# Convolving two entering chunks in one set of matmuls, with tiles of two for x and the partial sums

## The chip, the cores and the metric

The kernel runs on one core of a Trainium2 chip. The metric is the device time of one execution in microseconds. The kernel before takes 1448.68 us (median of three runs, 1447.93 to 1449.42).

## The reference

Two layers follow each other on `x` of shape (8, 4224, 192): batch `b`, token `s`, channel `d`.

```python
# 1: causal convolution along the tokens, 7 taps, one softmax-normalised set of taps per head (8 heads of 24 channels)
x = einsum('hk,bskhg->bshg', softmax(weight), windows_of_7(x))
# 2: phase layer
theta = x @ w_theta
zr, zi = x * cos(theta), x * sin(theta)
y = einsum('ts,bsd->btd', w_tok_r, zr) + einsum('ts,bsd->btd', w_tok_i, zi)
u = x + y
out = u + relu(u @ w_ch)
```

Nearly all of the work is the token mix `y`: two products of 4224 x 4224 matrices with 4224 x 1536 data.

## The kernel before

**Chunks and steps.** The tokens that are summed over (`s`) are cut into 33 chunks of 128 tokens; the tokens of the output (`t`) into 33 blocks of 128. A chunk lives in an fp16 tile `z` (7 parts of 768 columns, 11 buffers), so at most 11 chunks are resident and there are three rounds of 11 chunks. The main loop runs over 58 steps. A step takes one pair of output blocks (step 6, 23, 40 and 57 take a single one) and multiplies it with all resident chunks: for a pair, seven runs over the chunks (`runs`, `mix`), each with a transposed or summed weight tile `wt`, two matmuls of 384 columns per run and chunk (line 443), accumulated in PSUM tiles `y`. At the end of some runs `give` adds `y` into the partial sums `pv` (line 408, VectorE), which are fp32 tiles of 128 x 1536, one per output block. After a step its `pv` go to a DRAM scratch `part` (line 456), and a round later they are read back (`load_rows`, line 372). In the last round they stay until the output is made of them (`output`, line 476).

**Entering chunks.** `start` says at which step a chunk becomes resident. In rounds two and three the chunks enter at steps 18 to 23 and 36 to 41, two at a time, except for one that enters alone at step 20 and one at step 38. Each of these chunks is prepared in the step before it enters. Two steps before, at position 4.5 of the step's seven, `load_chunk` makes the tile `xw` and issues its loads: 96 partitions hold four token quarters with 16 rows of history each, so that there are four loads of x (line 197, POOL's queue, float32 to fp16) and, for every chunk but the first of a round, four copies of history out of the `xw` of the chunk before it (line 188, SP's queue). `conv` then convolves the chunk by matmuls with banded matrices (line 210): two calls, each with eight matmuls of 192 columns (four heads, two halves of the partitions) and one evacuation by ScalarE of 128 x 768 (line 151). Then come the transpose, the two `theta` calls and the VectorE products and sums.

**The order.** `pe`, `dve`, `act` and `pool` chain the instructions of an engine in the order in which the program issues them. `step_events` gives every side task of a step a position on a scale of seven, and `mix` issues it when the matmuls of the step get there. For the first of two entering chunks the two `conv` calls stand at 0.1 and 0.6, for the second at 2.4 and 2.9. Loads of `xw` are not chained; the scheduler places them on POOL's queue, and its order is fixed at build time. An instruction that waits on a queue holds all that stand behind it on the same queue.

**The buffers.** `xw` and `pv` share one set of six buffers (tag "big", 6144 bytes on each partition); only the `pv` of steps 0 and 1 live elsewhere. A new tile gets a buffer whose old tile has been released, and its first write waits for the last readers of the old tile.

```python
self.xw = wk.tile([2 * WR, 2, B, D], F16, name="xw", tag="big", bufs=6)    # line 182
pv = wk.tile([P, N], F32, name="pv", tag="big", bufs=6)                   # line 370
found.append((1.6, steps[t + 1].load_rows))                               # line 518
found.append((4.5, lambda k=k: load_chunk(k)))                            # line 542, k that start at t + 2
```

Of the kernel before, what the change touches and what calls it, by code (L numbers as in the profile page):

```python
# [11 lines left out]
F16 = mybir.dt.float16  # L12
F32 = mybir.dt.float32
# [3 lines left out]
def kernel(  # L17
# [23 lines left out]
    nc = tc.nc  # L41
    B, S, D = x.shape
    H, KS = weight.shape
    G = D // H
    P = nc.NUM_PARTITIONS
    assert (B, D, P) == (8, 192, 128) and S % P == 0
    N = B * D
    HD = D // 2
    HN = N // 2
    NQ = 4  # L50
    Q = P // NQ
    NK = S // P
    NT = S // P
    HALO = 16
    WR = Q + HALO
# [5 lines left out]
    NW = 11  # L61
# [4 lines left out]
    start = [base[k % NW] + (NU + 1) * (k // NW) for k in range(NK)]  # L66
# [17 lines left out]
    def pe(ins):  # L84
        return in_order("pe", ins)

    def dve(ins):
        return in_order("dve", ins)

    def act(ins):  # L90
        return in_order("act", ins)

    def pool(ins):
        return in_order("pool", ins)

    constp = ctx.enter_context(tc.tile_pool(name="const", bufs=1))
    wk = ctx.enter_context(tc.tile_pool(name="wk", bufs=2))
    zpool = ctx.enter_context(tc.tile_pool(name="zpool", bufs=NW))
# [10 lines left out]
    xs = dram.tile([S, N], F16, name="xs")  # L109
    part = [dram.tile([NT, P, N], F32, name=f"part{i}") for i in range(2)]  # L110

    def banks(name, dtype=F32):
        return mmpool.tile([P, 2, PC if dtype == F32 else 2 * PC], dtype,
                           name=name, tag="mm")
# [5 lines left out]
    bands = constp.tile([2 * WR, H, 2, Q], F16, name="bands")  # L120
# [10 lines left out]
    def token(k, a):  # L131

        return (a * NK + k) * Q
# [13 lines left out]
    def evacuate(out, in_, by_dve=False):  # L147
        if by_dve:
            dve(nc.vector.tensor_copy(out=out, in_=in_))
        else:  # L150
            act(nc.scalar.activation(out=out, in_=in_, func=AT.Copy))  # L151
# [23 lines left out]
    Z11, T1, Z21, Z22, T2, T4, T3 = range(7)  # L175

    class Chunk:


        def __init__(self, k, before=None):  # L180
            self.k = k
            self.xw = wk.tile([2 * WR, 2, B, D], F16, name="xw", tag="big", bufs=6)
            for a in range(NQ):
                h, lo = a // 2, (a % 2) * WR
                t0 = token(k, a)
                hist = self.xw[lo : lo + HALO, h, :, :]
                if before is not None:
                    nc.sync.dma_start(
                        out=hist, in_=before.xw[lo + Q : lo + Q + HALO, h, :, :]
                    )  # L190
                elif t0 == 0:
                    nc.vector.memset(hist, 0.0)
                else:
                    lo, t0 = lo - HALO, t0 - HALO
                lo += HALO
                n = (a % 2 + 1) * WR - lo
                nc.gpsimd.dma_start(  # L197
                    out=self.xw[lo : lo + n, h, :, :],
                    in_=x[:, t0 : t0 + n, :].rearrange("b s d -> s b d"),
                )  # L200

        def conv(self, j):

            if j == 0:
                self.z = zpool.tile([P, 7, HN], F16, name="z", tag="z")
                self.x = self.z[:, T2 : T2 + 2, :].rearrange("p t n -> p (t n)")
            pc = banks("pc")
            for h in range(4):
                for half in range(2):
                    pe(nc.tensor.matmul(  # L210
                        pc[half * 2 * Q : (half + 1) * 2 * Q, h // 2,
                           h % 2 * B * G : (h % 2 + 1) * B * G],
                        lhsT=bands[:, 4 * j + h, :, :].rearrange("p a m -> p (a m)"),
                        rhs=self.xw[:, half, :, (4 * j + h) * G : (4 * j + h + 1) * G],
                        start=True, stop=True,
                    ))
            evacuate(
                self.x.rearrange("p (b d) -> p b d", d=D)[
                    :, :, 4 * j * G : 4 * (j + 1) * G
                ].rearrange("p b (i h g) -> p i h b g", i=2, h=2),  # L220
                pc[:, :, 0 : 2 * B * G].rearrange("p i (h b g) -> p i h b g", h=2, b=B),
                self.k == 0 and j == 1,
            )
            if j == 1:
                for a in range(NQ):
                    t0 = token(self.k, a)
                    nc.sync.dma_start(
                        out=xs[t0 : t0 + Q, :], in_=self.x[a * Q : (a + 1) * Q, :]
                    )

        def transpose(self):
            self.xT = turned()
# [27 lines left out]

        def tasks(self):

            for j in range(2):
                yield lambda j=j: self.conv(j)
            yield self.transpose
            for g in range(NG):
                yield lambda g=g: self.theta(g)
            yield lambda: self.product(Z11)
            yield lambda: self.product(Z21)
            yield lambda: self.sums(0)  # L270
            yield lambda: self.sums(1)

    chunks = {}

    def load_chunk(k):
        if k < NK and k not in chunks:
# [8 lines left out]
    class Step:  # L285
# [79 lines left out]
        def load_rows(self):  # L365
            for tb in self.tbs:
                if self.t < 2:
                    pv = zpool.tile([P, N], F32, name="pv", tag="z")
                else:
                    pv = wk.tile([P, N], F32, name="pv", tag="big", bufs=6)  # L370
                if not self.first:
                    nc.sync.dma_start(
                        out=pv, in_=part[(self.t // NU - 1) % 2][tb, :, :]
                    )
                self.pv.append(pv)
# [137 lines left out]
    def step_events(t):  # L513
        found = []
        s = steps[t]
        if t + 1 < NSTEP:
            found += steps[t + 1].w_tasks()
            found.append((1.6, steps[t + 1].load_rows))
            for i in steps[t + 1].adds:
                found.append((2 + 2 * i, lambda i=i: steps[t + 1].load_x(i)))  # L520
                found.append((3.6 + 2 * i, lambda i=i: steps[t + 1].add_x(i)))
        here = [(r, i, which) for r in steps for i, when, which in r.ahead if when == t]
        for j, (r, i, which) in enumerate(here):
            found.append((1.5 + 1.8 * j, lambda r=r, i=i, which=which: r.add_ahead(i, which)))
        if t + 2 < NSTEP:
            nxt = steps[t + 2]
            for m in (1, 2):
                found.append((1.3 + 3 * (m - 1), lambda m=m: nxt.load_w(m)))
        if t == NU - 2:
            def load_wch():  # L530
                dve(nc.vector.memset(wch[:, 1:3, :], 0.0))
                for rows, i, part_w in channel_pieces(moe_w_ch):
                    pool(nc.gpsimd.dma_start(out=wch[rows, i, :], in_=part_w))
            found.append((3, load_wch))
        for at, f in outputs:
            begin = at - sum(s.time for s in steps[:t])
            if 0 <= begin < steps[t].time:
                found.append((7 * begin / steps[t].time, f))
        if t >= NU - 2:
            new = [k for k in range(NK) if start[k] == t + 2 and k >= NW]  # L540
            for k in new:
                found.append((4.5, lambda k=k: load_chunk(k)))
            at = 0.1
            for k in (k for k in range(NK) if start[k] == t + 1 and k >= NW):
                pos = [0, .5, 1.4, 2.2, 2.6, 3.1, 3.15, 3.4, 3.6]

                def add(at, j, k):
                    def go():
                        if j == 0:
                            chunks[k].todo = chunks[k].tasks()  # L550
                        next(chunks[k].todo)()
                    found.append((at, go))
                for j, p in enumerate(pos):
                    add(at + p, j, k)
                at += 2.3
        return found
# [12 lines left out]
    for a in range(2):  # L569
        nc.gpsimd.affine_select(  # L570
            out=sel, in_=sel, pattern=[[1, Q - 1 + 2 * WR]], channel_multiplier=-1,
# [4 lines left out]
    for a, lo in ((0, True), (1, False)):  # L576
        nc.gpsimd.affine_select(
            out=block[:, a : a + 1], in_=block[:, a : a + 1], pattern=[[0, 1]],
# [7 lines left out]
    def idle(n):  # L586
# [7 lines left out]
        out=wmax, in_=wsb, axis=mybir.AxisListType.X, op=ALU.max  # L594
    ))
    dve(nc.vector.tensor_tensor(
        out=wsb, in0=wsb, in1=wmax[:, :].unsqueeze(2).to_broadcast([P, H, KS]),
# [6 lines left out]
        out=wsum, in_=wsb, axis=mybir.AxisListType.X, op=ALU.add  # L604
# [5 lines left out]
        out=wdiag, in0=wsb[0:KS, :, :],  # L610
# [4 lines left out]
        out=wcol, in_=wdiag, axis=mybir.AxisListType.X, op=ALU.add  # L615
# [5 lines left out]
    for q in range(Q):  # L621
        pe(nc.tensor.matmul(
            bp[0 : 2 * WR, 0, q * H : (q + 1) * H],
            lhsT=sel[:, Q - 1 - q : Q - 1 - q + 2 * WR], rhs=taps,
            start=True, stop=True,
# [3 lines left out]
        out=bands, in0=bv.unsqueeze(2).to_broadcast([2 * WR, H, 2, Q]),  # L629
# [32 lines left out]
    for i in range(NW + 2):  # L662
        ch = chunks.get(i) if i < NW else None
# [80 lines left out]
```

## Time and profile before

| | before |
|---|---|
| median of three runs | 1448.68 us |
| span of the profiled execution, first to last instruction | 1444.6 us |
| what lies around the span (median less span) | 4.1 us |
| TensorE busy (PE) | 1414.5 us, 98% of the span |
| VectorE (DVE), ScalarE (ACT), GpSimd (POOL) busy | 978.2, 316.2, 434.6 us |
| matmuls of the token mix, line 443 | 7656, start to start 0.163 us |
| matmuls of the convolution, line 210 | 528 |
| mean granted TensorE clock | 0.997 |

The span is one profiled execution; its own time was not measured apart, so the median less the span stands for what lies around it. In the views, PE is TensorE's matmuls and PEld its weight loads, which overlap them; SPq is SP's DMA queue. A line of the timeline gives start, duration, engine, line, operation, output tile from input tile, count, and in brackets the idle time of the engine before it and what ended it. A step of 11 chunks takes 25.0 us in round two; the steps 17 to 22 and 35 to 39, in which chunks are prepared, take 26.7 us.

### The profile page before, as it was taken

How to read it: one execution, taken by the hardware profiler on the slowest of the kernel's cores; microseconds unless marked ns; L12 is line 12 of the kernel's file. 1: busy time of each engine (PE TensorE's matmuls, PEld its weight loads, DVE VectorE, ACT ScalarE, POOL GpSimd, SP SyncE). 2: the span in 40 equal slices, each digit the busy share in tenths (PEclk: the TensorE clock that was granted, in tenths of full speed). 3: DMA queues.
4: the chain of work that ended last, by engine and by line, in shares of the span. 5: the costliest groups of instructions: out<-in, count | busy, mean ns of one | idle time of the engine just before them, and what ended most of it. 6: DMA issues, size and time to landing. Idle time of an engine off the chain costs nothing.

```text
span 1444.6 us, 23749 instructions
## 1 busy us (share of the span) xinstructions
PE 1414.5 (98%) x9809; PEld 886.3 (61%) x9809; DVE 978.2 (68%) x1050; ACT 316.2 (22%) x379; POOL 434.6 (30%) x655
## 2 busy tenths in 40 slices
PE   7899999999999999999999999999999999999997
PEld 4656666666666666666666666666666666666665
DVE  6893554555448687866666657876877677767686
ACT  6851101111124254000000004435210110010133
POOL 8421211111223232432433343233323123213120
PEclk9999999999999999999999999999999999999999
DMA  9975756564699999897899889989999999898883
GB/s 181 253 148 136 146 119 133 98 152 87 152 229 210 226 244 222 219 265 173 223 245 222 233 155 239 235 181 237 274 220 202 213 204 221 204 200 193 166 232 116
DMA packets 272029, 281.99 MB, mean 195 GB/s; under 512 B 106672, under 2 KB 240176, under 8 KB 271920
## 3 DMA queue, kind: packets, MB, share of 16 engines
q0 software_dynamic: 162464, 92.15, 48.4%
q1 hardware_dynamic: 71824, 178.88, 35.2%
q10 hardware_dynamic: 37632, 9.44, 4.3%
q8 instruction: 77, 1.26, 0.4%
q14 instruction: 32, 0.26, 0.1%
HBM read 245.49 MB, written 108.13 MB: 245 GB/s over the span
## 4 chain that ended last, share of the span: by engine, by line
PE 89%; DVE 3%; DMA 2%; ACT 2%; POOL 1%; issue 1%; SPq 0%; DVEq 0%; ACTq 0%; POOLq 0%
PE y L443 81%; PE v L141 5%; PE pc L210 1%; PE tp L165 1%; ACT z L246 1%; DVE pv L408 1%; DMA xw<-xw 1%; POOL xw L197 1%; DMA xw<-in_x_dram 1%; DVE z L257 1%; POOL st L323 1%; DVE z L251 1%; DMA pv<-part 1%; ACT uT L151 1%; DVE wt L336 0%
## 5 line engine op out<-in xcount | busy, mean ns | idle before, releaser
L443 PE MATMUL y<-z,wt 128*128 128x384 f16 x7656 | 1283.6, 326 | 10.4 <-DVE pv L408 7.3
L443 PEld LDWEIGHTS <-wt 128*128 128x128 f16 x7656 | 740.7, 98 | 488.1 <-issue 10.2
L408 DVE TENSOR_TENSOR pv<-y,pv 128x768 f32<-128x768 f32 x324 | 309.2, 955 | 327.0 <-PE y L443 286.8
L336 DVE STREAM_TRANSPOSE wt<-st 128x1408 f16<-128x1408 f16 (+7 forms) x224 | 327.8, 1465 | 45.8 <-PE y L443 39.1
L323 POOL DMA_DIRECT2D st<-in_moe_w_tok_r_dram x232 | 132.4, 579 | 464.9 <-DVE wt L336 459.4
L323 POOL DMA_DIRECT2D st<-in_moe_w_tok_i_dram x232 | 132.5, 580 | 405.4 <-DVE wt L336 397.5
L348 DVE TENSOR_TENSOR wt<-wt 128x1408 f16<-128x1408 f16 (+7 forms) x216 | 176.1, 815 | 40.5 <-PE y L443 38.0
L151 ACT ACTIVATE z<-pc 128x768 f16<-128x768 f32 x65 | 53.3, 820 | 386.7 <-PE pc L210 386.5
L151 ACT ACTIVATE ub<-pv 128x768 f16<-128x768 f32 x63 | 50.2, 835 | 333.2 <-DVE pv L408 310.7
L406 ACT ACTIVATE pv<-y 128x768 f32<-128x768 f32 x66 | 54.0, 819 | 281.6 <-PE y L443 281.6
L141 PEld LDWEIGHTS <-uT 128*128 128x128 f16 x1056 | 91.1, 98 | 27.4 <-issue 8.5
L386 POOL TENSOR_TENSOR pv<-pv,xr 128x1536 f32<-128x1536 f32 x24 | 74.5, 3105 | 67.1 <-DVE pv L476 21.9
L197 POOL DMA_DIRECT2D xw<-in_x_dram x132 | 76.5, 591 | 30.1 <-DMA xw<-xw 9.7
L476 DVE SCALAR_TENSOR_TENSOR pv<-v,pv 128x768 f32<-128x768 f32 x66 | 62.9, 954 | 27.5 <-PE v L141 27.0
L151 ACT ACTIVATE uT<-tp 128x1536 f16<-128x1536 f16 (+1 forms) x49 | 59.7, 1221 | 74.4 <-PE tp L165 74.4
L257 DVE TENSOR_TENSOR z<-z 128x768 f16<-128x768 f16 x132 | 73.4, 556 | 3.6
L246 ACT ACTIVATE z<-v,half_pi 128x768 f16<-128x768 f32 x66 | 59.9, 907 | 42.1 <-PE v L141 41.7
L251 DVE TENSOR_TENSOR z<-z 128x1536 f16<-128x1536 f16 x66 | 60.1, 948 | 6.6 <-ACT z L246 6.6
L141 PE MATMUL v<-wth,uT 128*128 128x192 f16 x528 | 55.0, 248 | 5.6 <-ACT z L246 3.3
L141 PE MATMUL v<-wch,uT 128*128 128x192 f16 x528 | 54.2, 246 | 2.1 <-DVE pv L476 1.2
L246 ACT ACTIVATE z<-v 128x768 f16<-128x768 f32 x66 | 53.5, 810 | 0.0
L210 PE MATMUL pc<-xw,bands 96*64 96x192 f16 x528 | 35.3, 256 | 1.2 <-DVE bands L628 0.8
(43 smaller groups left out, 138.0 us busy)
## 6 DMA issues: line engine op xcount, KB each, us to landing
part<-pv SPq DMA_DIRECT2D x79, 768.0 KB, 4.6
pv<-part SPq DMA_DIRECT2D x79, 768.0 KB, 6.0
out_dram<-pv SPq DMA_DIRECT2D x66, 384.0 KB, 4.3
st<-in_moe_w_tok_r_dram POOLq DMA_DIRECT2D x136, 176.0 KB, 5.7
st<-in_moe_w_tok_i_dram POOLq DMA_DIRECT2D x136, 176.0 KB, 5.1
xs<-z SPq DMA_DIRECT2D x132, 96.0 KB, 4.1
xw<-in_x_dram POOLq DMA_DIRECT2D x121, 96.0 KB, 5.9
xr<-xs SPq DMA_DIRECT2D x24, 384.0 KB, 4.5
```

The lines of the kernel that those rows point to most:

```text
L141: pe(nc.tensor.matmul(v[:, k, b * D : (b + 1) * D], lhsT=tT[:, 3 * k + b + i, :], rhs=w[:, 2 * b + i, :], start=(i == 0), stop=(i == 1),))
L151: act(nc.scalar.activation(out=out, in_=in_, func=AT.Copy))
L197: nc.gpsimd.dma_start(out=self.xw[lo : lo + n, h, :, :], in_=x[:, t0 : t0 + n, :].rearrange("b s d -> s b d"),)
L246: act(nc.scalar.activation(**args))
L251: dve(nc.vector.tensor_tensor(out=o, in0=xv, in1=o, op=ALU.mult))
L257: dve(nc.vector.tensor_tensor(out=z[:, o, :], in0=z[:, a, :], in1=z[:, b, :], op=ALU.subtract))
L323: pool(nc.gpsimd.dma_start(out=st[a * Q : (a + 1) * Q, 0:nb, :, 0:n] .rearrange("i r bt s -> i (r bt) s"), in_=w[self.tbs[0] * P : (self.t ...
L336: dve(nc.vector.transpose(self.w[name][:, 0 : self.n, :, :], self.st[int(name[1])][:, int(name[0]) - 1, :, 0 : self.n * Q] .rearrange("p b ...
L348: dve(nc.vector.tensor_tensor(out=self.w[name][:, 0 : self.n, :, :], in0=self.w[a][:, 0 : self.n, :, :], in1=self.w[b][:, 0 : self.n, :, : ...
L386: ins = pool(nc.gpsimd.tensor_tensor(out=self.pv[i], in0=self.pv[i], in1=self.xr[i], op=ALU.add))
L408: dve(nc.vector.tensor_tensor(out=o, in0=yv, in1=o, op=ALU.add))
L443: pe(nc.tensor.matmul(y[cn][:, q, 0:BH], lhsT=self.w[wn][:, c, :, :].rearrange("p bt i -> p (bt i)"), rhs=chunks[k].z[:, zn, q * BH : (q + ...
```

## The change

`xw` tiles now hold two chunks and `pv` tiles the two output blocks of a step, in three buffers of twice the size. A chunk that enters alone and a step with a single output block take a whole tile of two and use half of it. Where two chunks enter together, `conv_both` convolves them by matmuls over both, 384 columns each: four calls at positions 0.1, 0.45, 0.8 and 1.15, each with four matmuls (two heads, two halves) and two evacuations of 128 x 384, one for each chunk. The positions of the transposes and of all later tasks of the two chunks stay. Round one convolves each chunk by itself as before, out of tiles of two.

```diff
-            self.xw = wk.tile([2 * WR, 2, B, D], F16, name="xw", tag="big", bufs=6)
+            if k not in pairs:
+                both = wk.tile([2 * WR, 2, 2, B, D], F16, name="xw", tag="big", bufs=3)
+                pairs[k] = pairs[mate(k)] = (both, k)
+            self.both, first = pairs[k]
+            self.xw = self.both[:, :, k - first, :, :]
...
+        def conv_both(self, other, j):
+
+            if j == 0:
+                self.open()
+                other.open()
+            pc = banks("pc")
+            for h in range(2):
+                for half in range(2):
+                    pe(nc.tensor.matmul(
+                        pc[half * 2 * Q : (half + 1) * 2 * Q, h, 0 : 2 * B * G],
+                        lhsT=bands[:, 2 * j + h, :, :].rearrange("p a m -> p (a m)"),
+                        rhs=self.both[:, half, :, :, (2 * j + h) * G : (2 * j + h + 1) * G]
+                        .rearrange("p c b g -> p (c b) g"),
+                        start=True, stop=True,
+                    ))
+            for c, ch in enumerate((self, other)):
+                evacuate(
+                    ch.x.rearrange("p (b d) -> p b d", d=D)[
+                        :, :, 2 * j * G : 2 * (j + 1) * G
+                    ].rearrange("p b (h g) -> p h b g", h=2),
+                    pc[:, :, c * B * G : (c + 1) * B * G]
+                    .rearrange("p h (b g) -> p h b g", b=B),
+                )
+                if j == 3:
+                    ch.store()
...
         def tasks(self):
-            for j in range(2):
-                yield lambda j=j: self.conv(j)
+            if mate(self.k) == self.k and pairs[self.k][1] == self.k:
+                for j in range(2):
+                    yield lambda j=j: self.conv(j)
...
+    def mate(k):
+        near = [j for j in range(NK) if start[j] == start[k] and j // NW == k // NW]
+        if k < NW:
+            near = [j for j in range(k // 2 * 2, k // 2 * 2 + 2) if j < NW]
+        return near[-1]
...
-                    pv = wk.tile([P, N], F32, name="pv", tag="big", bufs=6)
+                    if not self.pv:
+                        both = wk.tile([P, 2, N], F32, name="pv", tag="big", bufs=3)
+                    pv = both[:, len(self.pv), :]
...
-            for k in (k for k in range(NK) if start[k] == t + 1 and k >= NW):
-                pos = [0, .5, 1.4, 2.2, 2.6, 3.1, 3.15, 3.4, 3.6]
+            new = [k for k in range(NK) if start[k] == t + 1 and k >= NW]
+            if len(new) == 2:
+                for j in range(4):
+                    found.append((0.1 + 0.35 * j, lambda j=j, new=new: chunks[new[0]]
+                                  .conv_both(chunks[new[1]], j)))
+            for k in new:
+                pos = [0, .5, 1.4, 2.2, 2.6, 3.1, 3.15, 3.4, 3.6][2 * len(new) - 2 :]
```

`open` and `store` are the old code for making `z` and for writing x to DRAM, moved into functions.

More of the change, by code (lines that the diff above doesn't have):

```diff
@@ L204, in conv @@
             if j == 0:
-                self.z = zpool.tile([P, 7, HN], F16, name="z", tag="z")
-                self.x = self.z[:, T2 : T2 + 2, :].rearrange("p t n -> p (t n)")
+                self.open()
             pc = banks("pc")
@@ L224, in conv, with open, store @@
             if j == 1:
[L225 to L229, printed above, removed]
+                self.store()
+        def open(self):
+            self.z = zpool.tile([P, 7, HN], F16, name="z", tag="z")
+            self.x = self.z[:, T2 : T2 + 2, :].rearrange("p t n -> p (t n)")
+        def store(self):
+            for a in range(NQ):
+                t0 = token(self.k, a)
+                nc.sync.dma_start(
+                    out=xs[t0 : t0 + Q, :], in_=self.x[a * Q : (a + 1) * Q, :]
+                )
+        def conv_both(self, other, j):
+            if j == 0:
+                self.open()
+                other.open()
[16 more added lines that the diff above has]
+                    .rearrange("p h (b g) -> p h b g", b=B),
+                )
+                if j == 3:
+                    ch.store()
         def transpose(self):
@@ L271, in tasks @@
             yield lambda: self.sums(1)
-    chunks = {}
+    chunks, pairs = {}, {}
+    def mate(k):
[3 more added lines that the diff above has]
+        return near[-1]
     def load_chunk(k):
```

## The prediction

> **What bounds the kernel now.** I read the page's busy times and groups first, then the stages one by one, then the timeline of one preparing step with its DMA issues. On the page TensorE is busy for 98% of the span, and nearly all of that is line 443; the convolution is 528 matmuls with 1.2 us of idle time before them.
>
> ```profile
> PE 1414.5 (98%) x9809; PEld 886.3 (61%) x9809; DVE 978.2 (68%) x1050; ACT 316.2 (22%) x379; POOL 434.6 (30%) x655
> L443 PE MATMUL y<-z,wt 128*128 128x384 f16 x7656 | 1283.6, 326 | 10.4 <-DVE pv L408 7.3
> L210 PE MATMUL pc<-xw,bands 96*64 96x192 f16 x528 | 35.3, 256 | 1.2 <-DVE bands L628 0.8
> ```
>
> The busy times by stage (columns: length, PE, PEld, DVE, ACT and POOL busy with counts, clock, DMA share, GB/s) show two stretches of the start and then a step that prepares a pair. In the last row PE has no idle time, so whatever holds PE there is paid in full. The first two are for the clock: after a stretch with PE busy 3.30 of 6 us, 4 us were granted 0.57.
>
> ```profile
> 30.00:36.00 6.00, 3.30 (x29) 1.60 (x26) 5.19 (x10) 4.97 (x7) 4.58 (x8) 1.00 1.17 185
> 36.00:40.00 4.00, 3.56 (x22) 2.31 (x23) 3.97 (x7) 1.51 (x3) 1.65 (x3) 0.57 1.31 248
> 893.60:920.30 26.70, 26.70 (x215) 17.17 (x214) 22.36 (x28) 12.34 (x14) 6.88 (x12) 1.00 1.05 251
> ```
>
> The timeline around the start of that step (step 36, at 893.6) shows when x is loaded and when it is used.
>
> ```profile
> 875.93 2.31 POOL L197 DMA_DIRECT2D xw<-in_x_dram  x4
> ...
> 887.76 2.41 SPq L188 DMA_DIRECT2D xw<-xw  x4
> ...
> 890.51 2.31 POOL L197 DMA_DIRECT2D xw<-in_x_dram  x4
> ...
> 893.27 2.25 SPq L456 DMA_DIRECT2D part<-pv  x2
> ...
> 893.99 0.52 PE L210 MATMUL pc<-xw,bands 96*64 96x192 f16 x8
> 894.22 0.95 DVE L408 TENSOR_TENSOR pv<-y,pv 128x768 f32<-128x768 f32 x1
> ...
> 903.26 0.52 PE L210 MATMUL pc<-xw,bands 96*64 96x192 f16 x8
> ```
>
> The first chunk's loads are issued 18 us before its convolution at 893.99, the second's 3.5 us before that; it is convolved only at 903.26. The step's last add into `pv` (894.22) and the store of that `pv` lie after 893.99.
>
> The DMA issues of the stage of steps 35 to 40 give KB each and median us from issue to landing:
>
> ```profile
> part<-pv SPq DMA_DIRECT2D x11, 768.0 KB, 5.3
> ...
> xw<-in_x_dram POOLq DMA_DIRECT2D x36, 96.0 KB, 7.7
> xw<-xw SPq DMA_DIRECT2D x36, 48.0 KB, 3.5
> ```
>
> **The matmuls.** Ten pairs lose 16 of 32 matmuls each, 160 in all. The chain of waits gives eight old ones 0.45 us. They run two at a time, one half into output partitions 0 to 63 and the other into 64 to 127, so 0.45 us are 4 x 192 = 768 columns; line 443 takes 315.10/1938 = 0.163 us for 384, thus 0.325 us for 768, and the remaining 0.12 us are the edges of the group. A new call is two such couples of 384: 768 columns again, and there are still four calls per pair. I take a gain of 0. If time went by instruction instead, it would be 160 x 0.45/8 = 9.0 us; a loss has no reason.
>
> **The evacuations.** ScalarE gets eight of 128 x 384 instead of four of 128 x 768 per pair. From 1.459 us for 128x1536 and 0.811 for 128x768 (line 151) I estimate 0.49 for 384; so 3.9 us instead of 3.3, on an engine busy 12.3 of 26.7 us. The transposes at 1.5 follow the last call at 1.15 by some 1.3 us of matmuls, and two evacuations take 1.0: I take 0.1 us a pair, bounds 0 and 0.5. The eight stores of x go together on SP's queue, behind the loads of the next `pv`; nothing near waits for them, and if something did, it would be 8 x 0.43 = 3.4 us.
>
> **The buffers.** This is the large part. At position 4.5 of step s-1 `load_chunk` asks for the x of the pair that enters at s+1. Three tiles of two are live then: the `pv` of s-1, which it still adds to; the `pv` of s, asked for at 1.6; and the x of the pair before, whose history the new pair copies. Before, the six single buffers came free one by one, and the first chunk got its own early. Now the new x must wait for both stores of the `pv` of s-1, at its very end, and the built order of the changed program does have the x loads behind these two stores. But the convolution stands at 0.1 of step s, in PE's fixed order, with the whole step's matmuls behind it. So PE waits from its 0.1 until stores, loads and copies are through:
>
> - from the convolution's place to the issue of the last store: 894.22 + 0.95 - 893.99 = 1.2 us;
> - the store: 5.3 us here, 4.6 over the whole run; I take 5.0, since no x loads run beside it now;
> - four loads issued in turn, the fourth 3 x 0.58 = 1.75 us after the first; landing 7.7 in this stage, 5.9 over the run; I take 5.6, as the four issued from 843.6 landed in 5.4 to 5.8, with little beside them;
> - SP's copies for the second chunk come out of the first chunk's tile: 0.1 to issue, 3.5 to land. The second chunk's own loads (fourth issued 7 x 0.58 = 4.1 after the start, landed at 9.7) are inside 1.75 + 5.6 + 0.1 + 3.5 = 10.95.
>
> A pair: 1.2 + 5.0 + 10.95 = 17.15 us. A lone chunk has four loads, and its copies come from an old tile: 1.2 + 5.0 + 1.75 + 5.6 = 13.55. Which steps: 18, 20, 21, 22 and 36, 38, 39, 40 for pairs, 19 and 37 for lone chunks. The first pairs of a round (prepared in steps 17 and 35) find a tile free; in step 35 three loads stand behind weight loads that were issued from 858.90 to 861.2, so they land at about 868.5 against 867.3: 1 us, bounds 0 and 3. Sum: 8 x 17.15 + 2 x 13.55 + 1 = 165.3 us. Nothing hides it: DVE and ACT run out of work within a few us, since all that they do next needs PE. What is queued behind: on POOL the weight loads of step s+2, needed a step later; on SP the `pv` loads of step s+1, also a step early. In the last round the `pv` loads come some 20 us ahead of their step even when both tiles wait for the later output.
>
> **The clock.** The row 36 to 40 gives 4 x (1 - 0.57)/0.5 = 3.4 us at half clock after much shorter gaps, which cost 1.7 us. I put 1.7 on each of the ten waits, 17.0 us; bounds 0.8 and 3.4. The Trainium skill, "TensorE: Matmul & The Clock Gate", part 1, states that an idle window of about 3.4 us halves the clock and that one busy window, free-running, restores it. That speaks against this change: by it I estimate 3.4 to 6.8 us at half clock per wait, 17 to 34 us in all. No row here shows a wait of 17 us.
>
> **Sum.** 165.3 + 17.0 + 8 x 0.1 = 183 us. On the span: 1444.6 + 183 = 1628; with the 4.1 us around it, 1632 us.
>
> **The rivals.**
> *Only the second chunk is late.* If x need not wait for `pv` (a release in parts, or a free buffer that I miss), there is still the second chunk's load, now needed about 9 us sooner. In the trace of before the last of its loads lands after the first chunk's convolution by 5.2, 4.1, 8.1, 3.8 us in round two and 9.0, 3.0, 3.4, 0 in round three: 36.6 us, with some half clock 40, so 1489. For it: the buffers did come free singly. Against: one tile has one release.
> *Slower still.* At the slow rows every wait is 1.5 + 6.7 (store) + 1.75 + 9 (loads) + 4.5 (copies) = 23.5 us, 19 for a lone chunk: 8 x 23.5 + 2 x 19 + 34 = 260, so 1709. For it: DMA share is 1.00 in this stage. Against: during the wait little else is moving.
> *Faster.* Matmuls priced by count give 9 us, 1440, if x were there in time. It decides when the loads land before position 0.1, that is when buffers are free about 11 us before the step ends. Against: the three live tiles above, and 768 columns either way.
>
> **How the numbers follow.** The forecast has 0.85, the second chunk's lateness 0.06, slower still 0.07, faster 0.02. The forecast's own bounds: quiet ends 1.0 + 3.3 + 1.75 + 4.0 + 3.0 = 13 for a pair and 10.5 alone, clock 8: 133 us, 1582; slow ends 20 and 16.5, clock 26, evacuations 4: 223 us, 1672. I widen the range towards both neighbours, to 1565 and 1690. A measurement of this kernel tells about 0.2%, 2.9 us, from no change; every case but the last is slower by more than that. Faster 0.02, same 0.01, slower 0.97.
>
> **What would show it.** After the change: idle time of PE before the new convolution matmuls of about 160 us in ten waits, ended by copies or loads of x; POOL's x loads waiting for `part<-pv`; the preparing steps 40 to 46 us long; a granted clock of about one half after each wait; the busy time of line 443 up by those slow stretches only. Wrong if x loads are issued before the step's last store, if the waits are below 13 or above 20 us, or if rows of 128x384 matmuls of the convolution take clearly less than half of the old time per pair.

## The result and the profile after: 12% slower

| | before | after |
|---|---|---|
| median of five runs | 1448.40 us (1447.65 to 1449.42) | 1626.43 us (1619.4 to 1628.36) |
| ratio | | 1.122, 95% interval 1.120 to 1.1235 |
| span of the profiled execution | 1444.6 us | 1617.7 us |
| TensorE busy, and the rest of the span | 1414.5, 30.1 us | 1438.8, 178.9 us |
| mean granted clock | 0.997 | 0.947 |

The profiled execution of the changed kernel was the quickest of the five, 1619.4 us; the spans of the five go from 1617.7 to 1626.6 us.

From the page of the kernel after: the busy times, the 40 slices of PE and of its clock, and two groups (busy, mean ns, idle time before them and what ended it).

```profile
PE 1438.8 (89%) x9649; PEld 886.0 (55%) x9649; DVE 976.0 (60%) x1050; ACT 320.6 (20%) x419; POOL 434.0 (27%) x655
PE   7999999999966665999999996655599999999997
PEclk9999999999988777999999998877899999999999
L489 PE MATMUL y<-z,wt 128*128 128x384 f16 x7656 | 1298.2, 328 | 12.7 <-DVE pv L454 9.0
L249 PE MATMUL pc<-xw,bands 96*64 96x384 f16 x160 | 28.4, 392 | 125.1 <-DMA xw<-xw 62.5
```

Two notches in PE and in its clock are the whole difference: rounds two and three begin there. PE was 98% busy before and is 89% now. Its idle time grew by 178.9 - 30.1 = 148.8 us, and its busy time by 1438.8 - 1414.5 = 24.3 us, though it executes 160 matmuls fewer: that is the lower clock, since half clock lasted 52 us in all behind the ten waits below, which is worth some 26 us. The two are the 173.1 us that the span grew by. The idle time stands before line 249, the new convolution.

The list of PE's waits (us in total, times, longest) names what ended them.

```profile
PE pc L249 <- DMA xw<-xw: 62.5, 10, 15.5
PE pc L249 <- DMA st<-in_moe_w_tok_r_dram: 48.3, 4, 16.5
PE pc L213 <- DMA xw<-in_x_dram: 22.7, 4, 10.1
PE pc L249 <- DMA xw<-in_x_dram: 14.1, 1, 14.1
```

The second line is to be read with care: the convolution reads no `st`, so the name cannot be right. These four waits stand before the same matmul as the others, which reads x, its history and the constant `bands`. The four lines sum to 147.6 us. They are ten long gaps, one in each of the ten late steps, of 13.8 to 16.5 us for a pair and of 9.1 and 10.1 us for a lone chunk, and nine short ones right behind them, where the first matmul had its data and the next had not.

The timeline of step 36 of the changed kernel, which starts at 980.1, shows the chain. The whole of it is new.

```profile
980.09 2.25 SPq L502 DMA_DIRECT2D part<-pv  x2
981.04 0.95 DVE L454 TENSOR_TENSOR pv<-y,pv 128x768 f32<-128x768 f32 x1
985.65 7.51 SPq L192 DMA_DIRECT2D xw<-xw  x8
986.27 4.54 POOL L201 DMA_DIRECT2D xw<-in_x_dram  x8 [8.92 <-DMA part<-pv]
994.84 0.50 PE L249 MATMUL pc<-xw,bands 96*64 96x384 f16 x1 [14.24 <-DMA xw<-xw]
...
998.85 0.52 PE L249 MATMUL pc<-xw,bands 96*64 96x384 f16 x4
```

The last add of the old step ends at 981.99, its store follows, POOL's x loads wait for that store until 986.27, and the matmul resumes at 994.84 after 14.24 us of nothing. In the trace of before the first chunk's loads were issued 18 us ahead of the convolution; here they come 5.7 us behind its place. The profile puts this wait down to `part<-pv` in only some of the steps, but the landings show it in all: in each of the ten late steps the first x load is issued 0.5 to 1.1 us after the step's second store has landed.

The busy times of that step, and of 4 us stretches around the resumption (columns as in the prediction: length, five engines, clock, DMA share, GB/s):

```profile
980.10:1023.80 43.70, 28.90 (x198) 17.04 (x198) 22.64 (x28) 12.79 (x18) 9.09 (x16) 0.84 0.67 145
...
992.00:996.00 4.00, 1.00 (x4) 0.31 (x4) 0.00 (x0) 0.00 (x0) 0.00 (x0) 0.50 1.17 225
996.00:1000.00 4.00, 4.00 (x19) 1.62 (x18) 0.00 (x0) 1.47 (x4) 0.00 (x0) 0.66 0.73 300
1000.00:1004.00 4.00, 4.00 (x35) 2.11 (x34) 2.38 (x2) 2.02 (x5) 0.00 (x0) 1.00 0.05 13
```

The step is 17.0 us longer than before, of which PE is idle for 14.8 and busy for 2.2 more. Between 996 and 1000 PE is busy all the time and yet issues 19 matmuls, where the next 4 us hold 35, some of them short transposes. The DMA share over the step is 0.67 where it was 1.05, so the step as a whole is not short of bandwidth; from the first x load to the resumption, though, the share is 1.05 too (142 GB/s), and whether bandwidth counts there is left to the experiments. The steps of the other pairs grew by 17.1 to 20.3 us, those of the lone chunks by 13.2 and 13.7, step 35 by 0.3 and the steps outside by at most 0.7.

### The profile page after: what moved, and what is told of

The parts are those of the page before. It is cut to its first block, busy times and chain, and to the rows that moved or that the text cites. A ratio compares the mean times of both kernels' runs of the same rounds, so it can differ in the third digit from the quotient of the medians.

```text
span 1617.7 us, 23448 instructions
## 1 busy us (share of the span) xinstructions
PE 1438.8 (89%) x9649; PEld 886.0 (55%) x9649; DVE 976.0 (60%) x1050; ACT 320.6 (20%) x419; POOL 434.0 (27%) x655
## 4 chain that ended last, share of the span: by engine, by line
PE 75%; DVE 9%; DMA 8%; issue 3%; ACT 2%; POOL 2%; SPq 0%; DVEq 0%; POOLq 0%; ACTq 0%
PE y L489 69%; PE v L141 4%; DMA xw<-in_x_dram 3%; DVE pv L454 2%; DMA xw<-xw 2%; DVE z L287 2%; DVE z L293 2%; PE pc L249 1%; DMA part<-pv 1%; DVE wt L380 1%; DVE wt L392 1%; POOL xw L201 1%; PE tp L165 1%; DMA xs<-z 1%; ACT z L282 1%
## 5 line engine op out<-in xcount | busy, mean ns | idle before, releaser
L489 PE MATMUL y<-z,wt 128*128 128x384 f16 x7656 | 1298.2, 328 | 12.7 <-DVE pv L454 9.0
L151 ACT ACTIVATE z<-pc 128x384 f16<-128x384 f32 (+1 forms) x105 | 55.7, 570 | 569.0 <-PE pc L249 519.9
L249 PE MATMUL pc<-xw,bands 96*64 96x384 f16 x160 | 28.4, 392 | 125.1 <-DMA xw<-xw 62.5
L249 PEld LDWEIGHTS <-bands 96*64 96x64 f16 x160 | 7.1, 116 | 143.3 <-issue 140.9
```

Of the source, the lines that this page charges most:

```text
L489: pe(nc.tensor.matmul(y[cn][:, q, 0:BH], lhsT=self.w[wn][:, c, :, :].rearrange("p bt i -> p (bt i)"), rhs=chunks[k].z[:, zn, q * BH : (q + ...
```

## The experiments

My theory: the tile of two makes the x loads wait for the end of the old step, which costs PE an idle stretch and then some us at half clock; the matmuls over both chunks gain nothing. The rivals: the convolution of the second chunk moved forward is what costs; the time is bandwidth; matmuls are priced by count; or asking for x earlier would have been enough.

### One part alone: the tiles

The changed kernel with the old convolution calls, 192 columns each at the old positions.

```diff
-            if mate(self.k) == self.k and pairs[self.k][1] == self.k:
-                for j in range(2):
-                    yield lambda j=j: self.conv(j)
+            for j in range(2):
+                yield lambda j=j: self.conv(j)
...
-            if len(new) == 2:
-                for j in range(4):
-                    found.append((0.1 + 0.35 * j, lambda j=j, new=new: chunks[new[0]]
-                                  .conv_both(chunks[new[1]], j)))
...
-                pos = [0, .5, 1.4, 2.2, 2.6, 3.1, 3.15, 3.4, 3.6][2 * len(new) - 2 :]
+                pos = [0, .5, 1.4, 2.2, 2.6, 3.1, 3.15, 3.4, 3.6]
```

> The tiles of two in three buffers, with the old convolution: two calls of eight matmuls of 192 columns per chunk, at the old positions. Theory (the x of an entering pair waits for both stores of the step's partial sums): the first chunk of each late group waits as a lone chunk did after the change, 9.1 to 10.1 us idle plus some 2.6 us at half clock, and so in ten steps; the second chunk, convolved some 9 us later, finds its data there. 10 x 13 = 130 us, so about 1580 us. Rival (the merged matmuls or their place at the start of the step cause the loss): about 1448 us, as before.

Measured: 1587.64 us, ratio 1.094 (1.089 to 1.099). The tiles alone cost 138.7 us. There are ten long waits again, of 9.2 to 11.4 us, with ten short gaps behind them:

```profile
PE pc L213 <- DMA xw<-in_x_dram: 112.7, 20, 11.4
```

The wait is shorter than in the changed kernel because the first chunk's convolution needs only the first chunk's four loads, not the copies for the second.

### One part alone: the order

The kernel before with its six single tiles; both chunks of a pair are convolved at 0.1, 0.45, 0.8 and 1.15, still with 192 columns a matmul.

```diff
+            if len(new) == 2:
+                for j in range(4):
+                    found.append((0.1 + 0.35 * j, lambda j=j, new=new: chunks[new[0]]
+                                  .conv_both(chunks[new[1]], j)))
...
+                    for half in range(2):
+                        pe(nc.tensor.matmul(
...
+                            rhs=ch.xw[:, half, :, (2 * j + h) * G : (2 * j + h + 1) * G],
```

> Single tiles in six buffers as before, but both chunks convolved in the four calls at 0.1 to 1.15, by matmuls of 192 columns. Theory: buffers come free one by one again, so the first chunk's x is there; the second chunk's last load is late by what the trace of before shows, 0 to 9 us in eight steps, 36.6 us in sum, and some half clock after the longer ones, so about 1485 to 1493 us; PE's idle time before the convolution 25 to 45 us in all. Rival (calling both chunks early is itself the loss): about 1620 us. Rival (nothing but the tiles matters): 1448 us.

Measured: 1482.61 us, ratio 1.023 (1.018 to 1.027): 33.6 us, 2 below the range. The lateness of the second chunk is a real cost, the one that the prediction's first rival priced at 36.6 to 40 us. The waits are smaller than expected, 17.4 us in all instead of 25 to 45, and the longest is 3.6 us:

```profile
PE pc L251 <- DMA xw<-in_x_dram: 17.4, 10, 3.6
```

The rest is on the busy side: PE's busy time rises by 15.8 us (1414.5 to 1430.3) at the same number of matmuls, with half clock behind several of these short waits (some 4 us of it come at the start, before any pair). So the rival's sum came out near, but of other parts than it was made of.

Tiles alone and order alone sum to 172.3 us; the whole change cost 178.0. So the order adds its share to the tiles' in the changed kernel too: there a pair's long wait is 15.0 us on average against 10.0 with the tiles alone.

### Taking away what holds the tile: own history, and an earlier request

Three tiles are live when x is asked for, and one of them is the old x, kept for the history that the new pair copies out of it. In the next kernel every chunk of rounds two and three loads its own history from DRAM (48 rows a load instead of 32), so that the old tile is free after its convolution.

```diff
-            chunks[k] = Chunk(k, before=chunks[k - 1] if k % NW else None)
+            chunks[k] = Chunk(k, before=chunks[k - 1] if k % NW and k < NW else None)
```

> The changed kernel, but in rounds two and three each chunk loads its own history from DRAM (48 rows per quarter instead of 32) in place of copying it out of the tile of the chunk before. Theory: the tile of the pair before is then free as soon as it is convolved, early in the step before, so the new x needs no tile of partial sums and the waits of 14 to 16 us go; left is the last of the eight loads, which stands on POOL's queue behind weight loads that end some 3 us before the step does: waits of 0 to 4 us in eight steps, so 1450 to 1480 us. Rival (the copies and the length of the load chain make the wait, not the buffer): only the copies' 3.6 us go, in eight steps, so about 1597 us.

Measured: 1470.33 us, ratio 1.014 (1.010 to 1.018). Of 178 us, 21 are left, in steps 18 (+2.8), 20 (+10.4), 36 (+3.2) and 38 (+7.1); waits of 0 to 4 us were expected, and the longest is 7.2. The timeline before the worst of them, step 20, shows POOL's queue:

```profile
495.87 2.28 POOL L367 DMA_DIRECT2D st<-in_moe_w_tok_i_dram  x4 [5.97 <-DVE wt L380]
498.14 0.62 POOL L201 DMA_DIRECT2D xw<-in_x_dram  x1
...
508.82 0.85 PE L249 MATMUL pc<-xw,bands 96*64 96x384 f16 x3 [7.21 <-DMA xw<-in_x_dram]
```

The last load of x stands behind weight loads that wait for VectorE. That is a place in a queue, not a tile, so in the next two kernels x is asked for at 3.0 instead of 4.5: once with own history, and once in the changed kernel as it is.

```diff
-                found.append((4.5, lambda k=k: load_chunk(k)))
+                found.append((3.0, lambda k=k: load_chunk(k)))
```

> Own history as in the run e3_own_history, and the loads of x at position 3.0 instead of 4.5, so that all eight stand on POOL's queue ahead of the step's second set of weight loads. Theory: they land before the step ends, no wait is left, and the merged matmuls stand alone: 1446 to 1452 us, same as before. Rival (merged matmuls are worth something by count, 160 x 0.056 us): about 1440 us. Rival (with tiles of two the new x still has to wait for partial sums in some steps, whatever its position): above 1460 us.

Own history and 3.0: 1450.07 us, ratio 1.0013 (1.0003 to 1.0023). No wait before the convolution is left; the page gives

```profile
PE 1418.5 (98%) x9649; PEld 881.6 (61%) x9649; DVE 978.7 (68%) x1050; ACT 320.5 (22%) x419; POOL 438.4 (30%) x655
```

> The changed kernel with x asked for at position 3.0 of the step instead of 4.5, and nothing else. My theory: the request stands behind the stores of the old partial sums because three tiles of two are live, so that asking earlier changes nothing; PE's order is the same, and the x loads still stand behind the second store of part<-pv in nine of ten preparing steps. I expect 1620 to 1632 us, pair waits of 13.8 to 16.5 us as before. Rival: what made the own-history kernel whole was the earlier position rather than the shorter life of the old tile; then this kernel loses its waits too and takes 1450 to 1480 us.

3.0 alone: 1623.27 us, ratio 1.121 (1.119 to 1.123), which is not clear of the changed kernel's 1.120 to 1.1235. The earlier position is worth nothing that can be measured while the old tile is held. PE waits as before, and POOL's x loads wait for the same store:

```profile
983.42 2.25 SPq L502 DMA_DIRECT2D part<-pv  x2
...
989.75 4.54 POOL L201 DMA_DIRECT2D xw<-in_x_dram  x8 [9.09 <-DMA part<-pv]
998.32 0.50 PE L249 MATMUL pc<-xw,bands 96*64 96x384 f16 x1 [14.39 <-DMA xw<-xw]
```

The life of the old x tile is thus the cause: without it the time falls by 156 us. The earlier position brings 20 us more then. The kernels with own history read more of x from DRAM than the changed kernel (144 KB a load instead of 96), so bandwidth is not what was missing. A fourth tile of two, which should also let x in early, was not tried.

### Are merged matmuls worth anything?

With no waits left, the matmuls over both can be compared with single ones. The kernel with own history and 3.0, with every matmul of 384 columns split into two of 192:

```diff
-                for half in range(2):
...
-                        rhs=self.both[:, half, :, :, (2 * j + h) * G : (2 * j + h + 1) * G]
-                        .rearrange("p c b g -> p (c b) g"),
...
+                for c in range(2):
+                    for half in range(2):
...
+                            rhs=self.both[:, half, c, :, (2 * j + h) * G : (2 * j + h + 1) * G],
```

> As the run e5_own_early, but each matmul over both chunks is split again into two of 192 columns, one for each chunk: 160 matmuls more, everything else the same. Theory (a matmul's time goes by its columns, here two at a time): within 1 us of e5_own_early. Rival (time goes by the number of matmuls): 9 us slower than e5_own_early.

Measured: 1450.18 us, ratio 1.0019 (1.0006 to 1.0033), with 160 matmuls more. The groups of the two kernels, 384 columns first:

```profile
L249 PE MATMUL pc<-xw,bands 96*64 96x384 f16 x160 | 20.6, 338 | 0.0
```

```profile
L250 PE MATMUL pc<-xw,bands 96*64 96x192 f16 x320 | 20.8, 252 | 0.0
```

Twice the instructions, 20.8 us for 20.6. Time goes by columns here; the 9 us by count are not there.

The kernel before with own history, its single tiles and single convolutions kept (the edit of own history and nothing else):

> The kernel before, with the history of the chunks of rounds two and three loaded from DRAM (48 rows a load instead of 32) instead of copied out of the tile before; six single tiles and single convolutions. Nothing in the kernel before waits for x, so I expect the time of before within 0.2%, 1446 to 1451 us. Rival: the old copies, which tie a tile to its neighbour, cost something that does not show as a wait; then it falls by 3 us or more, below 1445, and the history and not the pairing would explain part of what the repaired paired kernel reached.

Measured: 1447.31 us, ratio 0.9988 (0.9980 to 0.9997). It is 1.5 us below the kernel before that was measured beside it, within the 0.2% that the prediction allows a measurement of this kernel. No kernel with the pairing beats it.

### The clock's share

The idle stretch and the half clock after it are two terms. To part them, 80 matmuls of 384 columns on constants, whose sums are overwritten, stand in the changed kernel ahead of the first convolution call of the eight late pairs. At 0.163 us each they fill 13.0 us of a wait that is idle anyway.

```diff
             pc = banks("pc")
+            if j == 0 and start[self.k] not in (start[NW], start[2 * NW]):
+                for _ in range(80):
+                    pe(nc.tensor.matmul(
+                        pc[:, 0, 0:BH], lhsT=ident, rhs=wth[:, 0:2, :].rearrange("p i d -> p (i d)"), start=True, stop=True,
+                    ))
```

> The changed kernel with 80 more matmuls of 384 columns (13.0 us, of a constant, into the PSUM tile that the convolution then overwrites) ahead of the first call of each of the eight late pairs. The result is unchanged. Theory: they fill the wait, which is 13.8 to 16.5 us there, and keep the clock at full speed; the half clock after those eight waits (3.9 to 7.1 us, half of it lost, about 20 us in sum) goes: about 1606 us. The two lone chunks keep theirs. Rival (the slow matmuls after a wait have another cause): 1626 us. If the wait were not for data but for PE's own queue, the 80 matmuls would add: 1626 + 8 x 13 = 1730 us.

Measured: 1626.68 us, ratio 1.122 (1.118 to 1.1265): no gain, a miss, and the number of the rival. The profile speaks for the theory all the same. The filling ended a little early:

```profile
PE pc L213 <- DMA xw<-in_x_dram: 22.2, 4, 10.1
PE pc L254 <- DMA xw<-xw: 15.9, 9, 3.5
PE pc L254 <- DMA st<-in_moe_w_tok_r_dram: 11.2, 4, 3.8
```

In seven of the eight steps gaps of 2.2 to 3.8 us were left, and half clock lasted 3.6 to 9.1 us after them; in the eighth, step 18, it lasted 3.3 us after gaps of 0.7 and 1.4 us. That is 44 us in all, no less than in the changed kernel (41 us), so the half clock was not taken away. So the same with 96, 15.6 us:

> As the run e4_warm with 96 matmuls (15.6 us) ahead of the first call of each late pair, since in e4_warm some 2.2 to 3.5 us of the wait were left empty and the clock was half again after them for 3.6 to 9.1 us. The result is unchanged. Theory (the half clock comes from PE's idle time, and 2 us of it in a window of 3.4 us are enough): idle gaps below 1 us, no half clock after the eight pairs, some 20 us less and at most 8 us more where the matmuls run past the data: 1606 to 1615 us. Rival (half clock after a wait has another cause than idle time): 1627 to 1635 us.

Measured: 1617.34 us, ratio 1.117 (1.115 to 1.119), 9 us less than the changed kernel and 2 above the range expected. Half clock is gone after seven of the eight pairs (step 40 kept a gap of 2.7 us). In step 36 of this kernel (starting at 977.8) PE resumes at 993.77 at full clock:

```profile
992.00:996.00 4.00, 4.00 (x28) 1.86 (x25) 0.00 (x0) 0.87 (x2) 0.00 (x0) 1.00 0.90 308
```

The half clock behind the eight pairs' waits lasted 41 us in all in the changed kernel and so cost some 20. The gain stays below that, in part because 96 matmuls overrun the data where the wait was under 15.6 us (5.6 us in all, by the waits of the changed kernel): here PE resumes 16.0 us after the step's start, in the changed kernel 14.7. The rest is not accounted for; single executions of the two kernels spread by 5 to 9 us.

### Convolving later

If the data come 14 to 16 us into the step, later calls should hide them. The calls of the pairs go to 2.4 to 3.45, about 8 us later, and the later tasks with them.

```diff
-                    found.append((0.1 + 0.35 * j, lambda j=j, new=new: chunks[new[0]]
+                    found.append((2.4 + 0.35 * j, lambda j=j, new=new: chunks[new[0]]
...
+                if len(new) == 2:
+                    pos = [p + 2.3 - 1.4 * (k - new[0]) for p in pos]
```

> The changed kernel with the four calls of a pair at 2.4 to 3.45 instead of 0.1 to 1.15, and the two chunks' later tasks moved behind them (the second follows the first by 0.9). Tiles, loads and copies stay. Theory (the data come at a fixed time after the end of the step before, and what stands ahead of the wait in PE's order hides it): the calls stand 8.8 us of matmuls later, so the eight waits fall from 15.0 to about 6 us and the lone chunks' stay: some 70 us less than the changed kernel, 1540 to 1560 us. Rival (the loads are set off by the convolution's own place, so that the wait moves along): about 1626 us.

Measured: 1601.88 us, ratio 1.106 (1.104 to 1.108): 24.5 us less than the changed kernel, a miss by 40. On the pages idle time falls by 25.5 us (178.9 to 153.4) and busy time rises by 10.9 (1438.8 to 1449.7); that is 14.6 us and not 24.5, because the profiled execution was the quickest of the changed kernel and the slowest of this one. The timeline of step 36, which starts at 973.0 here:

```profile
976.03 0.32 SPq L502 DMA_DIRECT2D part<-pv  x1
...
979.97 4.56 POOL L201 DMA_DIRECT2D xw<-in_x_dram  x8 [14.25 <-DVE pv L454]
...
989.44 0.50 PE L249 MATMUL pc<-xw,bands 96*64 96x384 f16 x1 [8.60 <-DMA st<-in_moe_w_tok_r_dram]
...
991.40 0.82 PE L249 MATMUL pc<-xw,bands 96*64 96x384 f16 x3 [1.47 <-DMA st<-in_moe_w_tok_r_dram]
```

The store is issued 3.0 us after the step's start instead of 1.9, the x loads 7.0 instead of 6.2, and the first matmul runs at 16.4 instead of 14.7: VectorE's products, now later, push the old step's last adds. The wait in front of the first call did fall, from 15.0 us to 9.1 on average over the pairs. Part of it came back as second gaps (1.5 us in this fence, 1.2 to 3.7 us in the other seven pairs' steps), as 4.9 us in step 24, and as half clock, which lasted 6.6 to 10.2 us after the pairs' waits instead of 3.9 to 7.1. That each of these is due to VectorE's later work is argued, not shown.

## Why the prediction came out right

**The time.** 1632 was forecast and 1626.43 measured. The span forecast was 1628, against 1617.7 in the profiled execution and up to 1626.6 in the others. That it came this near is in part luck, as the terms below show.

**The buffers: mechanism right, size high.** The late request, its place behind the last store and the ten steps are as forecast, and the kernels with own history and with the earlier request show that the old tile's life is the cause. The waits were over-sized: short gaps included, 15.6 us a pair on average instead of 17.15, and 11.0 and 11.7 instead of 13.55 for the lone chunks. Two signs that the prediction named miss with them: the lone chunks' waits are below 13 us, and the late steps are 37.5 to 47.0 us long instead of 40 to 46 (the shortest, step 40, takes a single output block). In step 36 the first part held: 5.7 us from the convolution's place to the first x load, 6.2 forecast. The loads were over-sized. In place of 10.95 us, 8.9 us passed from the first load's issue to the landing of the last copy: the fourth load was issued after 1.7 us and took 4.5 to land, its copy followed within 0.1 and took 2.6. The first matmul runs at 994.84, after 8.6 us, because it needs only two of the four token quarters. The lone chunk of step 37 took 5.8 us in place of 7.35, its first matmul 3.8:

```profile
1030.58 2.29 POOL L201 DMA_DIRECT2D xw<-in_x_dram  x4 [9.56 <-issue]
1034.42 0.34 PE L213 MATMUL pc<-xw,bands 96*64 96x192 f16 x1 [10.08 <-DMA xw<-in_x_dram]
1036.42 0.85 PE L213 MATMUL pc<-xw,bands 96*64 96x192 f16 x7 [1.66 <-DMA xw<-in_x_dram]
```

The transfers of the stage say the same:

```profile
part<-pv SPq DMA_DIRECT2D x11, 768.0 KB, 3.7
xw<-in_x_dram POOLq DMA_DIRECT2D x36, 96.0 KB, 4.5
xw<-xw SPq DMA_DIRECT2D x36, 48.0 KB, 3.8
```

I had taken 5.6 us for a landing of x, from the four loads of before that were issued from 843.6; the median is 4.5, and the fourth load of the lone chunk landed 4.1 us after its issue. The reading of that row was wrong in two ways. These four belong to the first chunk of a round, which loads its own history, so they are half as large again as the loads of the late steps (96 KB); and the DMA share was 1.17 from 843.6 to 851.3, which is not "little beside them":

```profile
xw<-in_x_dram POOLq DMA_DIRECT2D x4, 144.0 KB, 5.5
```

A DMA time is to be carried over only from a transfer of the same size, and one read in a full stretch was too long here: the 96 KB loads took 7.7 us in that stage before and 4.5 after. Together with step 35 (0.3 us for 1) the forecast's 165.3 us were 148.8 of idle time.

**The clock: too cheap.** 17.0 us were forecast and 24.3 measured, in busy time. I had carried over 1.7 us from a much shorter stretch; half clock lasted 3.9 to 7.1 us after the waits of the changed kernel, 5.2 on average, which costs half of that.

The Trainium skill, "TensorE: Matmul & The Clock Gate", part 1, ties half clock to an idle window of about 3.4 us and full clock to a busy one of that length. The prediction's estimate from it was 17 to 34 us, and the 24.3 us lie in that; the estimate of 3.4 to 6.8 us at half clock for a wait was passed in one wait here (7.1 us), and in several waits of the experiments.

**Two errors cancel in part, by luck.** Idle time 16.5 us less than forecast and clock 7.3 more leave the span 10 us under. The median then lay 8.7 us above the profiled span, where the prediction put 4.1: only 1.7 us lie around that span, and the other 7 are the profiled execution being the quickest of the five.

**The matmuls and evacuations: right.** The gain of 0 holds, by 20.6 us against 20.8. The evacuations took 488 ns, 0.49 estimated, and nothing waits for them in the list.

**The rivals.** "Only the second chunk is late" was not an alternative but a part: 33.6 us by itself. "Slower still" took 9 us for the loads and 6.7 for the store; in the ten waits a load of x took 2.9 to 5.8 us and the last store 3.2 to 5.3. "Faster" needed the buffers, and with them there in time the result is still 1450 us, no gain.

The Trainium skill, "Perfetto Trace Analysis", "Optimization Strategy", says that the same gap repeating on the engine that should be saturated can mean that there is not enough SBUF or PSUM for the next tile. This trace is such a case, in SBUF: ten gaps of 9.1 to 16.5 us, gone when a tile is released, and the next asked for, earlier, with no memory added.

## What to carry to other kernels

When tiles that come free one by one are joined into one, list for the moment of each request which tiles are still held and by which last reader. A joined tile comes free only with the last reader of either half; the new request waits for the first tile that does, and asking earlier, by itself, did not help here. Removing that reader (here a copy out of the old tile, replaced by a slightly larger load) was worth 156 us, and filling or moving the wait 9 to 25. Joining matmuls gained nothing here, where the columns stayed the same.

## What was not expected of the hardware

- Short gaps are enough for the half clock. The filled kernels show it after gaps of 2.2 to 3.8 us, and once after two of 0.7 and 1.4 us, with 13 us of matmuls or more just ahead of them. One gap of 2.3 us, which every one of these kernels has at about 100 us, was followed by 3.6 to 4.1 us of half clock in four of them (tiles alone, order alone, own history and earlier, 96 matmuls) and by none in the other eight, the kernel before and the changed kernel among them. So the same gap can cost 2 us or nothing; what decides it, these runs do not show.
- Where second gaps follow the first, as in the kernel that convolves later, half clock went on longer: 6.6 to 10.2 us after the resumption, against 3.9 to 7.1 in the changed kernel. That the second gaps are the reason is not shown: with 3.0 alone it lasted 7.2 us after one wait whose second gap was only 1.0 us.
- Half clock costs on the busy side: the tiles alone raise PE's busy time by 32.1 us (1414.5 to 1446.6) at the same number of matmuls, more than the whole change did, although the waits are shorter. Half clock lasted 5.8 to 7.9 us after each of the ten long ones.
